# Second layer: its x prepared in eight steps over the block ahead, other places for its weights, two conversions per f, fewer remainders on GpSimd

## The chip, the cores and the metric

The kernel runs on one core of a Trainium2 chip. The metric is the time of one execution on the device in microseconds (us), median of three runs: 994.25 for the kernel before (991.24 to 998.31).

## What is computed

A two-scale attention feeds two feed-forward layers. All matrices are float32 (q, k, v of 4 x 8 x 576 x 64; 2304 tokens of width 512; first layer 512 to 1536 to 512 with a gate, second 512 to 2048 to 512).

```python
q_d = q.reshape(B, H, S // 4, 4, D).mean(axis=3)          # k_d and v_d alike
out_d = softmax(q_d @ k_d.T / 8) @ v_d                    # coarse
scores = where(abs(i - j) < 4, q @ k.T / 8, -1e9)         # a band of 7 keys
x = repeat(out_d, 4) + softmax(scores) @ v                # 2304 x 512
x = (sigmoid(x @ w_gate) * (x @ w_val)) @ w_out           # first layer
h = x @ w_in
out = (h * sigmoid(1.702 * h)) @ w_out2                   # second layer
```

## The kernel before

Each float32 product is made of three TensorE passes: an operand is split into a high part (a cast to the float32r format, on ScalarE) and a remainder (value minus high part, on VectorE or GpSimd), and high x high, remainder x high and high x remainder are summed in PSUM (`passes`, L777 to L779). `parts_of` (L721 and the cast at L719) makes the split and takes the engine of the remainder as an argument.

The tokens are in five blocks: four of 512 tokens, one per batch, and a fifth, E, of the 4 x 64 tokens left over, 256 wide. The first layer visits them in the order 0, 1, 2, E, 3, with the attention of the next batch beside blocks 0 to 2; the second in the order 0, 1, 2, 3, E. In the first layer one step of the loop over d_ff (an f, 128 columns) has a gate product, a value product (both into a PSUM tile `ph`), an evaluation (tanh on ScalarE, L820; the multiplication `th` on VectorE, L825, which reads PSUM), the split of the result (`ghi`, `glo`, L828 and L829), and the output product of the f before. Each f uses three weight tiles of 128 x 512, which are kept in SBUF from the first block on (ring `w`, 36 tiles) and split anew for each block into rings of four tiles, `whi` and `wlo`. `weights` (from L737) says which engine takes the remainder: in block E every other one VectorE and GpSimd, in block 3 VectorE for the output weights (part 2) and GpSimd for the rest.

In the second layer two f's go together (a pair; eight pairs per block) and the product x @ w_in of a block of 512 tokens is made with Strassen's seven products (`hidden2`). For this x is needed as seven sums of quarters, each with high part and remainder (t1, t3, t4, t6 in `xhi` and `xlo`; t7, b11, b22 in tiles `xe0` to `xe2`), and each pair of weight tiles as four pieces (s1; s5 and s2; a11 and a22; s6 and s7), sums at L872, L874 and L877 into the two buffers of ring `we`, and then split into `whi` and `wlo`. `load_x7` prepares the sums of x for a block at one time in the plan, in two halves (k = 0, 1): each reads two tiles of x from DRAM (`st`, two buffers, `x2d`), makes four sums into the tile `tails` (L1028, L1030) and one into a buffer of `we` (L1035) on VectorE, seven casts on ScalarE and seven remainders of 128 x 256 on GpSimd.

The weights arrive as 64 bit words and are converted on the chip (`bits`, L696 to L710): a DMA, a ScalarE operation into a buffer of `we` (L701), and three VectorE operations (L703, L705, L710). `convert2` does this for the second layer's 32 tiles: the 16 tiles of w_in into the ring `raw`, the 16 of w_out into places `w2`, with a split besides. `CONV` says at which f of the first layer's last two visits (E, then 3) which tile is converted; six of w_in are converted in the first three pairs of the second layer's block 0.

Places: the raw tiles `wr0` to `wr7` (`low`) lie under the last 16 of the first layer's 36 weight tiles, and `places` are tiles under the attention's tiles (14) and under the first 20 weight tiles (10), which come free when their first user has ended.

Nothing of the order is written by hand. `Plan.order` takes the operations with an engine, a cost and a due time each, and simulates the five queues: whichever engine is free next takes the operation with the earliest due time among those whose inputs it believes ready. The engines then run these lists in order, and wait on semaphores where an operation's inputs are late. The planner's cost of an operation does not depend on what another engine does at that time.

```python
def parts_of(m, hi, lo, due, eng, n=512):
    (rm, vm), (rh, vh), (rl, vl) = m, hi, lo
    op("act", act_ns(n), lambda: nc.scalar.copy(vh(), vm()), [rm], [rh], due)
    ns, on = (dve_ns(n), nc.vector) if eng == "dve" else (pool_ns(n), nc.gpsimd)
    op(eng, ns, lambda: on.tensor_sub(vl(), vm(), vh().bitcast(F32)), [rm, rh], [rl], due)
```

## Time and profile before

| | |
|---|---|
| median of 3 runs | 994.25 us (991.24 to 998.31) |
| the profiled execution: its time | 996.08 us |
| the profiled execution: its span | 993.9 us |
| granted TensorE clock, mean over the span | 0.974 of full speed |
| TensorE busy | 952.5 us, 96% |
| VectorE busy | 709.1 us, 71% |
| ScalarE busy | 509.8 us, 51% |
| GpSimd busy | 371.6 us, 37% |

PE is TensorE's matmuls, PEld its weight loads, DVE VectorE, ACT ScalarE, POOL GpSimd, SP the queue that issues the DMAs. Times of rows count from the start of the span. A matmul's end is modelled, so that consecutive ones overlap in the rows; what counts is the distance from start to start. A row of the timeline has start, duration, engine, line, operation, tiles (output <- inputs, without buffer numbers), shapes, count, and in brackets the idle time of the engine before it with what ended it. In the stages of the run the first layer's block E begins near 425 us, its block 3 near 482, the second layer near 573, and the second layer's blocks 1, 2 and 3 near 670, 760 and 850.

### The profile page before, as it was taken

Reading aid. Unit: us, or ns where it says so; the run is one execution under the profiler, and the core shown is the slowest. Engines: PE = TensorE matmul, PEld = TensorE weight load, DVE = VectorE, ACT = ScalarE, POOL = GpSimd, SP = SyncE. Lnnn points to the kernel's source line nnn. Section 1 sums busy time; section 2 is a strip of 40 time slices with the busy share of each in tenths; the row PEclk is TensorE's granted clock in tenths of the full one; section 3 lists DMA queues with packets and bytes.
Section 4 is the critical chain, followed back from the end, with each engine's and each line's share of the span. In section 5 each row is a group of like instructions: output and inputs, shape, how many; then the busy total and the mean of one; then the engine's idle time right before and its main releaser. Section 6 shows DMA issues by size and latency. Waiting matters only on the chain.

```text
span 993.9 us, 20546 instructions
## 1 busy us (share of the span) xinstructions
PE 952.5 (96%) x8188; PEld 808.3 (81%) x8188; DVE 709.1 (71%) x1326; ACT 509.8 (51%) x1156; POOL 371.6 (37%) x356
## 2 busy tenths in 40 slices
...
GB/s 212 189 124 198 206 166 190 96 53 81 26 1 123 89 2 2 22 137 14 127 22 168 108 106 85 1 22 65 1 12 12 64 1 22 64 1 1 4 40 22
DMA packets 34447, 71.50 MB, mean 72 GB/s; under 512 B 3448, under 2 KB 15152, under 8 KB 34352
## 3 DMA queue, kind: packets, MB, share of 16 engines
...
## 4 chain that ended last, share of the span: by engine, by line
PE 72%; DVE 16%; issue 4%; DMA 3%; ACT 3%; POOL 1%; SPq 0%; DVEq 0%; ACTq 0%; POOLq 0%
PE ph L777 11%; PE ph L778 10%; PE ph L779 10%; PE acc L777 9%; PE acc L779 9%; PE acc L778 9%; PE pa L778 3%; PE pa L779 3%; PE pa L777 3%; DVE we L705 2%; PE pa L639 2%; DVE w L903 1%; DVE tails L1030 1%; DVE wlo L721 1%; DMA st<-x2d 1%
## 5 line engine op out<-in xcount | busy, mean ns | idle before, releaser
L777 PE MATMUL ph<-xhi,whi 128*128 128x512 f32 (+1 forms) x544 | 200.8, 369 | 3.9 <-DVE th L825 2.7
L778 PE MATMUL ph<-xhi,wlo 128*128 128x512 f32 (+1 forms) x544 | 196.5, 361 | 0.0
L779 PE MATMUL ph<-xlo,whi 128*128 128x512 f32 (+1 forms) x544 | 195.9, 360 | 0.0
L721 POOL TENSOR_TENSOR wlo<-wr,whi 128x512 fp32r<-128x512 f32 x78 | 104.4, 1338 | 150.8 <-ACT whi L719 150.4
L721 POOL TENSOR_TENSOR wlo<-we,whi 128x256 fp32r<-128x256 f32 x64 | 68.2, 1065 | 155.6 <-PE pa L779 101.7
L777 PEld LDWEIGHTS ph<-xhi,whi 128*128 128x128 f32 x544 | 103.1, 190 | 26.1 <-issue 8.1
L778 PEld LDWEIGHTS ph<-xhi,wlo 128*128 128x128 f32 x544 | 103.3, 190 | 16.5 <-DVE wlo L721 0.7
L721 POOL TENSOR_TENSOR wlo<-w,whi 128x512 fp32r<-128x512 f32 x52 | 71.4, 1375 | 119.5 <-ACT whi L719 119.5
L779 PEld LDWEIGHTS ph<-xlo,whi 128*128 128x128 f32 x544 | 103.2, 190 | 15.6
L719 ACT CAST whi<-wr 128x512 fp32r<-128x512 f32 x128 | 78.6, 615 | 41.9 <-PE acc L779 16.0
L825 DVE SCALAR_TENSOR_TENSOR th<-th,ph 128x512 f32<-128x512 f32 (+1 forms) x68 | 41.1, 605 | 70.1 <-PE ph L779 56.5
L777 PE MATMUL acc<-ghi,whi 128*128 128x512 f32 (+1 forms) x232 | 87.3, 376 | 0.0
L779 PE MATMUL acc<-glo,whi 128*128 128x512 f32 (+1 forms) x232 | 85.5, 368 | 1.4 <-DVE glo L829 1.4
L719 ACT CAST whi<-w 128x512 fp32r<-128x512 f32 x100 | 61.2, 616 | 49.7 <-PE ph L779 19.2
L778 PE MATMUL acc<-ghi,wlo 128*128 128x512 f32 (+1 forms) x232 | 85.7, 369 | 0.8 <-DVE wlo L721 0.8
L719 ACT CAST whi<-we 128x512 fp32r<-128x512 f32 (+1 forms) x96 | 52.6, 548 | 62.9 <-DVE w L915 23.4
L820 ACT ACTIVATE th<-ph 128x512 f32<-128x512 f32 (+1 forms) x68 | 36.2, 532 | 61.9 <-PE ph L779 61.9
L778 PE MATMUL acc<-w,glo 128*128 128x512 f32 x144 | 56.9, 395 | 1.4 <-DVE glo L941 1.4
L779 PE MATMUL acc<-w,ghi 128*128 128x512 f32 x144 | 57.3, 398 | 0.0
L703 DVE TENSOR_SCALAR we<-we 128x512 int32<-128x512 int32 x68 | 37.8, 556 | 27.0 <-ACT we L701 26.8
L777 PE MATMUL acc<-w,w 128*128 128x512 f32 x144 | 56.9, 395 | 0.0
L778 PE MATMUL acc<-w,w 128*128 128x512 f32 x144 | 56.8, 394 | 0.0
(162 smaller groups left out, 2424.3 us busy)
## 6 DMA issues: line engine op xcount, KB each, us to landing
...
```

What stands on the lines that cost most here:

```text
L639: nc.tensor.matmul(s.t[h * D:(h + 1) * D, q:q + NQ], vt.t[ks, g, v0 + h * D:v0 + (h + 1) * D], tt.t[ks, h, g, :NQ], start=True, stop=True, ...
L703: op("dve", 335.0, lambda: nc.vector.tensor_scalar(e.t, e.t, 3, None, op0=ALU.logical_shift_left), [], [e], due)
L705: op("dve", 602.0, lambda: nc.vector.scalar_tensor_tensor(e.t, words(0), 29, e.t, op0=ALU.logical_shift_right, op1=ALU.bitwise_or), [w], [ ...
L719: op("act", act_ns(n), lambda: nc.scalar.copy(vh(), vm()), [rm], [rh], due)
L721: op(eng, ns, lambda: on.tensor_sub(vl(), vm(), vh().bitcast(F32)), [rm, rh], [rl], due)
L777: nc.tensor.matmul(o, lhi, rhi, start=first, stop=False, skip_group_check=more)
L778: nc.tensor.matmul(o, llo, rhi, start=False, stop=False, skip_group_check=more)
L779: nc.tensor.matmul(o, lhi, rlo, start=False, stop=last, skip_group_check=more)
L820: op("act", act_ns(n, True), lambda h=h: nc.scalar.activation(th.t[:, :n], h.t[:, :n], AF.Tanh, scale=0.5 if layer == 1 else 1.702 / 4.0), ...
L825: op("dve", dve_ns(n), lambda: nc.vector.scalar_tensor_tensor(th.t[:, :n], th.t[:, :n], 1.0, hb[-1].t[:, :n], op0=ALU.add, op1=ALU.mult), ...
L903: out=tq()[:, o], in0=b.t[:, :H], in1=tq()[:, in1], op=alu) if flip else nc.vector.tensor_tensor(
L1030: op("dve", dve_ns(H), lambda p0=p0, p1=p1, fn=fn, i=i, ff=ff: fn(ff()[:, i], p0[0]()[:, p0[1]], p1[0]()[:, p1[1]]), st, [(four, i)], at)
```

## The change

- `load_x7` becomes a generator with eight steps (two sums each, then the one in `we`, then the two halves of the tiles themselves, for k = 0 and 1). `visit` starts it at the first pair of the block ahead and sends it on once per pair; for block 0 of the second layer it starts at f = 2 of the first layer's block 3. Its DMAs lose their earliest time.
- Places: `low` now lies under the first 16 weight tiles of the first layer, whose last use is early in block 3. One set of the tiles `xe`, the two more `ghi`/`glo` buffers and nine of the w_out places are under the attention's tiles; the other set of `xe` and seven w_out places are under the later weights.
- `CONV`: three w_out tiles in block E instead of six; in block 3 all 16 w_in tiles and six of w_out, 22 over twelve f's, where 10 and 10 stood; the last seven w_out tiles one per pair in the second layer's block 0, where six w_in tiles stood in the first three pairs.
- Remainders: in block E all are on VectorE, in block 3 parts 1 and 2; GpSimd keeps block 3's gate weights.

```diff
--- before.py
+++ after.py
@@ -293,9 +293,9 @@
 
     NRAW = NF2 // 2
     NTOP = 3 * NF1 // 2 - NRAW
+    low = [wpools[0].tile([P, 2, 512], I32, name=f"wr{i}", tag=f"wr{i}") for i in range(NRAW)]
     top = [wpools[1].tile([P, 2, 512], I32, name=f"w{i}", tag=f"w{i}") for i in range(NTOP)]
-    low = [wpools[0].tile([P, 2, 512], I32, name=f"wr{i}", tag=f"wr{i}") for i in range(NRAW)]
-    wslots = [Slot(x[:, i]) for x in top + low for i in range(2)]
+    wslots = [Slot(x[:, i]) for x in low + top for i in range(2)]
     plan.ring("w", wslots)
     aslots = []
     for nm, n, shape in (("qt", 2, [P, S + 12]), ("kt", 2, [P, KPAD + S + 5]), ("vt", 2, [P, NG, VC]),
@@ -318,15 +318,16 @@
             late[side] = tc.alloc_tile_pool(name="w2" + side, bufs=1, side=side, reuse_waits="tile")
         return late[side].tile([P, 2, 512], F32R, name=f"w2_{i}", tag=f"w2_{i}")
 
-    places = [Slot(lambda i=i: second(i), aslots if i < NREG else wslots[:2 * NTOP]) for i in range(NREG + NTOP)]
-    plan.ring("raw", [Slot(x, wslots[2 * (NTOP + i):2 * (NTOP + i) + 2]) for i, x in enumerate(low)])
+    places = [Slot(lambda i=i: second(i), aslots if i < NREG else wslots[2 * NRAW:]) for i in range(NREG + NTOP)]
+    plan.ring("raw", [Slot(x, wslots[2 * i:2 * i + 2]) for i, x in enumerate(low)])
 
     NX, NGX = 3, 2
-    plan.ring("w2", places[:NREG] + places[NREG + 2 * NX + NGX:])
+    NR = NREG - NX - NGX
     for n in range(NX):
-        plan.ring(f"xe{n}", places[NREG + n:NREG + 2 * NX:NX])
+        plan.ring(f"xe{n}", [places[n], places[NREG + NF2 - NR + n]])
+    gplaces = places[NX:NX + NGX]
     plan.ring("ex", places[NREG - 2:NREG])
-    gplaces = places[NREG + 2 * NX:NREG + 2 * NX + NGX]
+    plan.ring("w2", places[NX + NGX:NREG + NF2 - NR])
 
     accs = ring("acc", 4, [P, 512], pool=ps)
     hs_ = ring("ph", 2, [P, 512], pool=ps)
@@ -403,9 +404,12 @@
     FIRST = ((-15.0e3, 0.0), (3.5e3, 0.0), (10.0e3, 8.0e3))
 
 
-    CONV = [[[f // 2] if f % 2 else [] for f in range(NF1)], [[f + 6] for f in range(NF1)]]
-    for f, raws in ((8, (0, 1)), (9, (2, 3)), (10, (4, 5, 6)), (11, (7, 8, 9))):
-        CONV[1][f] = [*[f + 6][:f < 10], *[NF2 + n for n in raws]]
+    CONV = [[[f // 3] if f % 3 == 2 and f < 9 else [] for f in range(NF1)], [[] for _ in range(NF1)]]
+    last = []
+    for p in range(NRAW):
+        last += [NF2 + 2 * p, NF2 + 2 * p + 1, *[p + 3][:p + 3 < NR]]
+    for n, x in enumerate(last):
+        CONV[1][n * NF1 // len(last)].append(x)
     NGROW = 7
     visits = []
     clock = T0
@@ -740,11 +744,8 @@
                 w32[f, part] = buf("w")
                 signed(*bits(1, f, part, t - 8000.0), w32[f, part], t - 8000.0)
             m = whole(w32[f, part], F32)
-            nsplit[0] += 1
             eng = "pool"
-            if vi["j"] == E:
-                eng = ("pool", "dve")[nsplit[0] % 2]
-            elif vi["j"] == 0 or part == 2:
+            if vi["j"] in (0, E) or part == 2 or vi["j"] == B - 1 and part:
                 eng = "dve"
         hi, lo = buf("whi"), buf("wlo")
         parts_of(m, whole(hi), whole(lo), t - 4000.0, eng)
@@ -997,7 +998,7 @@
                 r += c
                 pos += c
 
-    def load_x7(j, t):
+    def load_x7(j):
 
 
         H = 256
@@ -1011,36 +1012,57 @@
         for b, nm in zip(more, ("t7", "b11", "b22")):
             x7[nm] = [(b, n) for n in range(4)], lambda b=b: b.t[:, 0], lambda b=b: b.t[:, 1]
         for k in range(2):
-            at = t - 6000.0 + 2000.0 * k
+            c = slice(k * H, (k + 1) * H)
             st = [buf("st") for _ in range(2)]
-            for n in range(2):
-                dma(st[n].t, x2d[j].t[:, k + 2 * n], P * 4 * T, [(x2d[j], k + 2 * n)], [st[n]], at - 5000.0,
-                    at - 14000.0)
-            four, one = buf("four"), buf("we")
-            ff = lambda four=four: four.t
+            four = buf("four")
+            a, b = ((lambda n=n, st=st: st[n].t.rearrange("p (a c) -> p a c", c=H)) for n in range(2))
+
+            def summed(dst, v, p0, p1, fn, at):
+                op("dve", dve_ns(H), lambda: fn(v(), p0[0]()[:, p0[1]], p1[0]()[:, p1[1]]), st, [dst], at)
+
+            def extra(n, m, at):
+                z = more[n]
+                parts_of(m, ((z, k), lambda c=c: z.t[:, 0, c]), ((z, 2 + k), lambda c=c: z.t[:, 1, c]),
+                         at, "pool", H)
+
+            def minus(o, x, y):
+                nc.vector.scalar_tensor_tensor(o, x, -1.0, y, op0=ALU.mult, op1=ALU.subtract)
+
+            add, less = nc.vector.tensor_add, nc.vector.tensor_sub
+            for i, (p0, p1, fn) in enumerate((((a, 0), (b, 1), add), ((a, 1), (b, 1), less), ((b, 0), (a, 0), less),
+                                              ((a, 0), (a, 1), minus))):
+                if i % 2 == 0:
+                    at = yield
+                if i == 0:
+                    for n in range(2):
+                        dma(st[n].t, x2d[j].t[:, k + 2 * n], P * 4 * T, [(x2d[j], k + 2 * n)], [st[n]], at - 9000.0)
+                v = lambda i=i, four=four: four.t[:, i]
+                summed((four, i), v, p0, p1, fn, at)
+                parts_of(((four, i), v), ((xh, (k, i)), lambda c=c, i=i: xh.t[:, i, c]),
+                         ((xl, (k, i)), lambda c=c, i=i: xl.t[:, i, c]), at, "pool", H)
+            at = yield
+            one = buf("we")
             fo = lambda one=one: one.t.bitcast(F32)[:, :H]
-            a, b = ((lambda n=n, st=st: st[n].t.rearrange("p (a c) -> p a c", c=H)) for n in range(2))
-
-            c = slice(k * H, (k + 1) * H)
-            for i, (p0, p1, fn) in enumerate((
-                    ((a, 0), (b, 1), nc.vector.tensor_add), ((a, 1), (b, 1), nc.vector.tensor_sub),
-                    ((b, 0), (a, 0), nc.vector.tensor_sub),
-                    ((a, 0), (a, 1), lambda o, x, y: nc.vector.scalar_tensor_tensor(
-                        o, x, -1.0, y, op0=ALU.mult, op1=ALU.subtract)))):
-                op("dve", dve_ns(H), lambda p0=p0, p1=p1, fn=fn, i=i, ff=ff: fn(
-                    ff()[:, i], p0[0]()[:, p0[1]], p1[0]()[:, p1[1]]), st, [(four, i)], at)
-                parts_of(((four, i), lambda i=i, ff=ff: ff()[:, i]),
-                         ((xh, (k, i)), lambda c=c, i=i: xh.t[:, i, c]),
-                         ((xl, (k, i)), lambda c=c, i=i: xl.t[:, i, c]), at, "pool", H)
-            op("dve", dve_ns(H), lambda b=b, fo=fo: nc.vector.tensor_add(fo(), b()[:, 0], b()[:, 1]),
-               [st[1]], [one], at)
-            for z, m in zip(more, ((one, fo), (st[0], lambda a=a: a()[:, 0]), (st[1], lambda b=b: b()[:, 1]))):
-                parts_of(m, ((z, k), lambda z=z, c=c: z.t[:, 0, c]),
-                         ((z, 2 + k), lambda z=z, c=c: z.t[:, 1, c]), at, "pool", H)
+            summed(one, fo, (b, 0), (b, 1), add, at)
+            extra(0, (one, fo), at)
+            at = yield
+            extra(1, (st[0], lambda a=a: a()[:, 0]), at)
+            extra(2, (st[1], lambda b=b: b()[:, 1]), at)
+
+    steps = [None]
+
+    def step_x7(at):
+        if steps[0]:
+            try:
+                steps[0].send(at)
+            except StopIteration:
+                steps[0] = None
+
+    def start_x7(j):
+        steps[0] = load_x7(j)
+        next(steps[0])
 
     def load_x(layer, j, t):
-        if layer == 2 and j != E:
-            return load_x7(j, t)
         n = width(j)
         if layer == 1:
             xs[layer, j] = (buf("ex"), buf("ex"))
@@ -1081,6 +1103,11 @@
             else:
                 gh, gl, t = hidden(vi, f, t)
                 g = gh, gl
+
+            if (layer, j) == (1, B - 1) and f == 2 or layer == 2 and j < B - 1 and f == 0:
+                start_x7(j + 1 if layer == 2 else 0)
+            if (layer, j) == (1, B - 1) or layer == 2 and j < B - 1:
+                step_x7(t + 3000.0)
             if pend[0]:
                 t = pend[0](t)
             now[0] = t
@@ -1101,9 +1128,8 @@
                         for x in gplaces:
                             for n, nm in enumerate(("ghi", "glo")):
                                 plan.rings[nm][0].append(Slot(lambda x=x, n=n: x.t[:, n], x.under))
-                if vi["layer"] == 2 and vi["j"] == 0 and f + 11 < NF2:
-                    for n in range(2):
-                        convert2(NF2 + f + 10 + n, t + 1300.0)
+                if vi["layer"] == 2 and vi["j"] == 0 and NR + f // 2 < NF2:
+                    convert2(NR + f // 2, t + 1300.0)
                 return t
 
             pend[0] = fin
```

The planner's lists before and after, at three places. First VectorE at the second layer's step from block 0 to block 1. `wr_112` (before) and `wr_102` (after) are the first raw tile, whose pieces block 1's first pair needs; L874 and L875 sum the pieces s5 and s2 of a pair, and the remainder `wlo` behind is theirs; `th_97<-th_97,w_85` is the last evaluation of block 0. Before:

```order
L1035 TENSOR_TENSOR we_87<-st_101 128x256
L938 SCALAR_TENSOR_TENSOR th_97<-th_97,w_85 128x512
L941 TENSOR_TENSOR w_20_6026<-th_96,w_20_6026 128x512
L874 TENSOR_TENSOR we_86<-wr_113 128x512
L941 TENSOR_TENSOR w_21_6078<-th_97,w_21_6078 128x512
L874 TENSOR_TENSOR we_87<-wr_112 128x512
L721 TENSOR_TENSOR wlo_79<-we_87,whi_75 128x512
```

After:

```order
L904 TENSOR_TENSOR w_85<-w_85,pa_161 128x256
L875 TENSOR_TENSOR we_87<-wr_102 128x512
L904 TENSOR_TENSOR w_85<-w_85,pa_162 128x256
L878 TENSOR_TENSOR we_86<-wr_102 128x512
L725 TENSOR_TENSOR wlo_79<-we_87,whi_75 128x512
L939 SCALAR_TENSOR_TENSOR th_97<-th_97,w_85 128x512
L873 TENSOR_TENSOR we_87<-wr_103 128x256
L942 TENSOR_TENSOR w_4_6064<-th_97,w_4_6064 128x512
```

The remainder of the first pair's s5 and s2 stood behind the evaluation, two splits and another pair's sum; it now stands ahead of the evaluation.

GpSimd from the start of block E of the first layer (`w_13<-tails` are the remainders of E's own x; `w_1_4796` and the like are places of w_out; rows with `st` or `xlo` are the second layer's x). Before:

```order
L1065 TENSOR_TENSOR w_13_4763<-tails,w_12_4756 128x256 x4
L721 TENSOR_TENSOR wlo_79<-w_104,whi_75 128x512
L721 TENSOR_TENSOR w_1_4796<-we_87,w_1_4796 128x512
L721 TENSOR_TENSOR wlo_81<-w_103,whi_77 128x512
L721 TENSOR_TENSOR wlo_81<-w_105,whi_77 128x512
L721 TENSOR_TENSOR wlo_79<-w_106,whi_75 128x512
L721 TENSOR_TENSOR wlo_81<-w_107,whi_77 128x512
L721 TENSOR_TENSOR w_3_4953<-we_87,w_3_4953 128x512
L721 TENSOR_TENSOR wlo_79<-w_108,whi_75 128x512
L721 TENSOR_TENSOR wlo_81<-w_109,whi_77 128x512
L721 TENSOR_TENSOR wlo_79<-w_110,whi_75 128x512
```

After, down to the first remainder of block 3's weights, `wlo_81<-wr_102`:

```order
L1087 TENSOR_TENSOR w_13_4760<-tails,w_12_4753 128x256 x4
L725 TENSOR_TENSOR w_1_4844<-st_100,w_1_4844 128x256
L725 TENSOR_TENSOR w_2_4877<-st_101,w_2_4877 128x256
L725 TENSOR_TENSOR w_6_4900<-we_87,w_6_4900 128x512
L725 TENSOR_TENSOR xlo_90<-tails,xhi_88 128x256 x4
L725 TENSOR_TENSOR wlo_81<-wr_102,whi_77 128x512
```

The weights' remainders are gone from GpSimd here, and half of the x of the second layer's block 0 is prepared at this early place.

VectorE between two evaluations `th` of the first layer's block 3. Before, ahead of the evaluation of f = 7:

```order
L721 TENSOR_TENSOR wlo_80<-wr_113,whi_76 128x512
L710 SCALAR_TENSOR_TENSOR we_86<-w_82,we_86 128x512
L829 TENSOR_TENSOR glo_94<-th_96,ghi_92 128x512
L703 TENSOR_SCALAR we_87<-we_87 128x512
L721 TENSOR_TENSOR w_22_5760<-we_86,w_22_5760 128x512
L705 SCALAR_TENSOR_TENSOR we_87<-w_83,we_87 128x512
L710 SCALAR_TENSOR_TENSOR wr_112<-w_83,we_87 128x512
L703 TENSOR_SCALAR we_86<-we_86 128x512
L705 SCALAR_TENSOR_TENSOR we_86<-w_84,we_86 128x512
L710 SCALAR_TENSOR_TENSOR wr_112<-w_84,we_86 128x512
L703 TENSOR_SCALAR we_87<-we_87 128x512
L705 SCALAR_TENSOR_TENSOR we_87<-w_82,we_87 128x512
```

After, from f = 0 to the evaluation of f = 1:

```order
L725 TENSOR_TENSOR wlo_78<-wr_104,whi_74 128x512
L830 TENSOR_TENSOR glo_94<-th_96,ghi_92 128x512
L714 SCALAR_TENSOR_TENSOR wr_103<-w_84,we_86 128x512
L707 TENSOR_SCALAR we_87<-we_87 128x512
L709 SCALAR_TENSOR_TENSOR we_87<-w_85,we_87 128x512
L707 TENSOR_SCALAR we_86<-we_86 128x512
L980 TENSOR_SCALAR ev_99<-acc_158 128x256
L714 SCALAR_TENSOR_TENSOR wr_103<-w_85,we_87 128x512
L725 TENSOR_TENSOR wlo_80<-wr_105,whi_76 128x512
L709 SCALAR_TENSOR_TENSOR we_86<-w_82,we_86 128x512
L1021 TENSOR_TENSOR we_87<-st_101 128x256
L826 SCALAR_TENSOR_TENSOR th_97<-th_97,ph_160 128x512
```

Stretches of this length (twelve or thirteen instructions) stood ahead of the evaluations of f = 7, 8 and 9 before, with six to eight instructions in the others; in the list of the change eight of the nine from f = 0 to f = 9 have eleven to fourteen, and the last two have four and five.

## Rows read from the trace of the kernel before

**Rows 1.** The page, busy us (share of the span) and instructions of each engine

```profile
PE 952.5 (96%) x8188; PEld 808.3 (81%) x8188; DVE 709.1 (71%) x1326; ACT 509.8 (51%) x1156; POOL 371.6 (37%) x356
```

**Rows 2.** Windows by stage: length, busy us (instructions) of PE, PEld, DVE, ACT, POOL, PEclk

```profile
424.70:482.00 57.30, 55.31 (x428) 53.22 (x427) 50.58 (x67) 36.55 (x75) 33.38 (x24) 1.00 0.19 61
482.00:548.00 66.00, 66.00 (x293) 54.66 (x292) 44.58 (x64) 35.50 (x65) 29.14 (x23) 1.00 0.34 120
548.00:572.60 24.60, 20.72 (x89) 16.21 (x88) 22.17 (x28) 12.03 (x26) 18.60 (x17) 1.00 0.32 106
572.60:664.00 91.40, 84.24 (x500) 72.50 (x500) 84.61 (x150) 48.87 (x106) 36.81 (x33) 0.98 0.18 58
664.00:753.00 89.00, 86.24 (x526) 77.31 (x527) 68.54 (x133) 46.90 (x104) 40.19 (x40) 0.98 0.08 25
753.00:842.00 89.00, 86.62 (x531) 77.65 (x530) 69.06 (x133) 46.72 (x104) 40.21 (x40) 0.98 0.08 25
842.00:931.00 89.00, 85.27 (x531) 76.38 (x530) 64.13 (x127) 44.62 (x98) 34.88 (x33) 1.00 0.06 19
931.00:994.00 63.00, 57.77 (x344) 50.62 (x343) 29.23 (x51) 23.86 (x55) 9.07 (x7) 0.99 0.08 26
```

**Rows 3.** PE's timeline where the second layer's blocks 1, 2 and 3 begin

```profile
672.18 0.28 PE L778 MATMUL ph<-xhi,wlo 128*128 128x256 f32 x1
672.30 0.28 PE L779 MATMUL ph<-xlo,whi 128*128 128x256 f32 x1
674.78 0.39 PE L777 MATMUL pa<-w,whi 128*128 128x256 f32 x1 [2.20 <-ACT whi L719]
675.50 0.58 PE L778 MATMUL pa<-w,wlo 128*128 128x256 f32 x1 [0.34 <-DVE wlo L721]
675.88 0.41 PE L779 MATMUL pa<-w,whi 128*128 128x256 f32 x1
...
763.84 0.54 PE L777 MATMUL pa<-w,whi 128*128 128x256 f32 x1 [1.97 <-ACT whi L719]
...
853.83 0.39 PE L777 MATMUL pa<-w,whi 128*128 128x256 f32 x1 [3.04 <-ACT whi L719]
```

**Rows 4.** Timeline of DVE and ACT ahead of the stall at 674.78

```profile
669.87 0.68 DVE L938 SCALAR_TENSOR_TENSOR th<-th,w 128x512 f32<-128x512 f32 x1
...
671.63 1.23 DVE L874 TENSOR_TENSOR we<-wr 128x512 f32<-128x512 f32 x1
...
673.39 0.68 DVE L874 TENSOR_TENSOR we<-wr 128x512 f32<-128x512 f32 x1
...
674.11 0.62 ACT L719 CAST whi<-we 128x512 fp32r<-128x512 f32 x1 [2.60 <-DVE we L874]
```

**Rows 5.** DVE's timeline in the first layer's block 3

```profile
519.86 0.68 DVE L825 SCALAR_TENSOR_TENSOR th<-th,ph 128x512 f32<-128x512 f32 x1
...
528.01 0.68 DVE L825 SCALAR_TENSOR_TENSOR th<-th,ph 128x512 f32<-128x512 f32 x1
...
537.76 0.68 DVE L825 SCALAR_TENSOR_TENSOR th<-th,ph 128x512 f32<-128x512 f32 x1
538.36 0.69 DVE L721 TENSOR_TENSOR wlo<-wr,whi 128x512 fp32r<-128x512 f32 x1
...
540.62 1.67 DVE L705 SCALAR_TENSOR_TENSOR we<-w,we 128x512 int32<-128x512 int32 x1
...
549.52 0.68 DVE L825 SCALAR_TENSOR_TENSOR th<-th,ph 128x512 f32<-128x512 f32 x1
```

**Rows 6.** POOL's timeline at the same place

```profile
540.38 1.36 POOL L721 TENSOR_TENSOR w<-we,w 128x512 fp32r<-128x512 f32 x1 [4.95 <-ACT w L719]
541.69 1.75 POOL L721 TENSOR_TENSOR wlo<-wr,whi 128x512 fp32r<-128x512 f32 x1
```

**Rows 7.** The chain of waits ahead of block 1: start, us, what

```profile
659.70 2.90 DMA st<-x2d
```

**Rows 8.** Waits of ACT's conversions: us in total, times, longest

```profile
ACT we L701 <- DMA w<-w: 10.7, 6, 5.7
```

## The prediction

> **What bounds the kernel now.** I read the page first: TensorE is busy for 952.5 of 993.9 us, no other engine for more than 71% [rows 1]. So the time is TensorE's, and a change that moves no matmul can only win where TensorE stands still. The windows by stage say where that is. From block E of the first layer to the end of the second layer's block 3 the length less PE's busy time is 2.0, 0.0 and 3.9, 7.2, 2.8, 2.4 and 3.7 us: together 22.0 [rows 2]. The stretch before 424.7 us is hardly touched by the change, and of the 5.2 us after 931 most is the last output's way out.
>
> The idle time of the rows is not all that a stall costs. At the start of the second layer's block 1 the matmuls go 0.12 us from start to start (672.18, 672.30); then come 674.78, 675.50 and 675.88 [rows 3]. That is 3.58 us for three that would take 0.36, so 3.2 lost, where the brackets say 2.20 and 0.34. I therefore price a us of idle time at 3.2 / 2.54 = 1.3 us.
>
> The same view, around the starts of blocks 2 and 3, shows stalls of 1.97 and 3.04 us, all three released by ACT's cast `whi` [rows 3]. What that cast waited for stands in the timeline of the other two engines: VectorE makes the last evaluation of block 0 at 669.87, then two splits and two sums L874, and only the second sum, at 673.39, is the one whose cast starts at 674.11 [rows 4]. It is the order that holds it back: both `we` buffers were taken, one by L1035 of x. Further back the chain of waits begins with a load of x, 2.90 us [rows 7].
>
> In block 3 of the first layer I read VectorE's evaluations `th`. They come 8.15 us apart (519.86, 528.01), which is TensorE's time for one f; at the end of the block 11.76 us apart (537.76, 549.52) [rows 5]. There the list has thirteen instructions instead of seven, and some are slow: L705 takes 1.67 us while GpSimd's remainder runs, where 0.69 us is usual for a wide one without it (L721 at 538.36) [rows 5, 6].
>
> **What GpSimd costs VectorE.** A wide (128 x 512) VectorE instruction takes 0.60 us from start to start (537.76 to 538.36) [rows 5]; for a narrow one, and for the shift L703, I take the 0.34 that follows if some 0.08 us of it does not depend on the width (an estimate). Between the same marks the list before has, in block E, 34 wide and 30 narrow: 30.6 us. VectorE was busy for 50.6, with three instructions more, and GpSimd for 33.4 [rows 2]: some 18 us too much, 0.5 us for each us of GpSimd. Block 3: 65 and 27, 48.2 us against 44.6 + 22.2, GpSimd 29.1 + 18.6: 0.39. Block 0 of the second layer: 67 and 80, 67.4 us (three more rows in the window) against 84.6, GpSimd 36.8: 0.44. These ratios hold whatever the mechanism is.
>
> The Trainium skill has the rule (SBUF — State Buffer, Who interferes with whom): a VectorE instruction with two SBUF inputs and a GpSimd instruction that reads SBUF want one port pair, and the loser is blocked for the winner's whole instruction. L705 against 0.69 us agrees. Taken to its end, each GpSimd us as a VectorE us, block 0 would need 67.4 + 36.8 = 104 us of VectorE before; the window measured 84.6, so half of the overlaps miss one another, and I keep the ratios.
>
> **The change part by part.** No matmul is added or taken away.
>
> *Boundaries in the second layer.* The list now has the first pair's remainder of s5 and s2 ahead of the last evaluation; it stood behind it, behind two splits and another pair's sum. The lists at the next two boundaries differ in the same way. The 2.20, 1.97 and 3.04 us should go, and most of what follows them. What is late next is GpSimd: the second half of x still ends in the last pair (three of its five sums, four of its remainders), among that pair's other remainders. I leave 1.5 of 8.9 us idle over the three blocks: 7.4 x 1.3 = 9.6 us won. Range: 11.6 (all) to 4.8 (half).
>
> *Block 3.* The list has 81 wide and 30 narrow instead of 65 and 27: 58.8 us, since remainders came from GpSimd, 16 instead of 10 raw tiles are converted (six more by three instructions) and four w_out tiles fewer. GpSimd has 23 instead of 44, 15 wide and 8 narrow; at 1.36 us for a wide one [rows 6] and 0.75 for a narrow one (an estimate, a little over half of it), that is 26 us, at 0.39 another 10. VectorE: 69 us, before 66.8, so it is no lighter, but even. The heaviest f has 7.0 us and about 0.9 from GpSimd, 7.9 of 8.15 us; before, three in a row had 7 us while GpSimd was busy 18.6 of 24.6 us. I take 1.5 us idle instead of 3.9: 3.1 us won. Range: 5.0 won to 3 lost, if the stretches of 7 us meet more than their share of GpSimd.
>
> *Block 0 of the second layer.* 66 wide and 80 narrow, 66.8 us, where 67.4 stood; GpSimd has 19 wide and 23 narrow instead of 16 and 18, 43 instead of 35 us, at 0.44 another 3.4 us for VectorE. So this block gets no lighter either: 66.8 + 0.44 x 43 = 86 us of its 8 x 11.1 (the starts of blocks 1 and 2 are 89.1 us apart [rows 3]). But its pairs, which had 11.2, 11.3, 6.4 and 10.7 us behind the first and then 7.0 to 8.5, now have 8.2, 9.7, 10.8, 5.8, 9.7, 9.5, 10.7 and 7.3. With GpSimd's share (1.9 us per pair before, 2.4 now) less 11.1, VectorE's lag, pair by pair, rose before to 2.0 and 4.1, on top of a first pair of 9.5 that met the end of block 3; now it is 0, 1.0, 3.1, 0.2, 1.2, 2.0, 4.0. Part of that is caught by what is ready ahead. I take 4.0 us idle instead of 7.2: 4.2 us won. Range: 8 won to 3 lost.
>
> *Block E.* GpSimd loses all 18 weight remainders and VectorE gets them: 47 wide and 32 narrow, 39.1 us instead of 30.6. With GpSimd down to seven instructions the total falls from 50.6 to some 42. But both halves of other work meet at the start: E's own four remainders, a conversion and half of the x for the second layer stand together, and VectorE's first five f's have 17.0 instead of 13.9 us against 5 x 4.1 of TensorE (half of 8.15). With 4 to 5 us from GpSimd that is 21 to 22 of 20.5. I add 1.0 us idle: 1.3 us lost. Range: 2 won to 4 lost.
>
> *At nothing.* The places as such: the same loads and stores. The x loads on SP's queue lose their earliest time; two go up in the list between the stores of the first layer's block 0, whose landing they wait for, with the next heads' q and k behind them. TensorE has attention and the weights of a whole block there; if that cover failed, one wait would cost at most about the 2.90 us of such a load [rows 7]. The others leave earlier than before, which removes that wait at the boundaries.
>
> **Sum.** 996.08 (the profiled execution, 993.9 of it span) - 9.6 - 3.1 - 4.2 + 1.3 = 980.5. This execution was 1.8 us over the median of the three runs, so the forecast is 978.7, in round figures 979.
>
> **Rivals.**
> 1. *Only the boundaries gain.* VectorE is as busy in blocks 3 and 0 as before, and if being even is worth nothing, only 9.6 is won and 1.3 lost: 994.25 - 8.3 = 986. For it: the total loads, 69 against 66.8 and 86 against 84.6. Against it: the stalls stood in the f's and pairs with most work, and none in 482 to 548 [rows 2].
> 2. *The x is still late.* The steps don't go where they are asked for: the planner takes x in two lumps, in pairs 2 to 3 and 6 to 7, and the last remainders are GpSimd's business at the boundary. Then half of the 9.6 stays: 978.7 + 4.8 = 983.5. Against it: the cast that released all three stalls doesn't wait for x.
> 3. *Slower: conversions block ScalarE.* In block 3 two conversions per f share two `we` buffers, with x's own sum besides, and ScalarE's conversion (L701) waits in order for a buffer or a load, with the casts `whi` of the weights queued behind it; TensorE waits for those. It waited for loads six times before, 10.7 us in all, 5.7 at the longest [rows 8]. With 22 conversions in a row, half of them holding ScalarE for that mean of 1.8 us with nothing in stock would cost 20 us and eat the 3.1: 978.7 + 23 = 1002. It decides from a wait of some 3 us on: four buffers `whi` hold a third more than the three tiles of an f, which is 8.15 / 3 = 2.7 us of work in stock. Against it: ScalarE is at 35.5 of 66 us there [rows 2].
>
> On the other hand the Trainium skill warns (Perfetto Trace Analysis, Optimizing Scalar/DVE Operations) that shifting work between VectorE and GpSimd may not help, as they share a read port. In block E the rows go against it: a remainder costs GpSimd over 1.3 us, hence VectorE some 0.7, and on VectorE 0.6; by the warning block E would be worth nothing, which is within its range.
>
> **Chances.** Forecast 0.61, the first rival 0.17, the second 0.15, the third 0.07. Measurements tell 1% from no change here, that is 984.3 and 1004.2. Faster: 0.57 of the forecast, 0.09 of the second rival, 0.05 of the first, 0.71. Slower by over 1%: about half of the third and a little of unseen things, 0.06. The rest, 0.23, is within 1%. The range: below, all stalls gone, 22.0 x 1.3 = 28.6, would be 966, and I stop at 967; above, rival 1 (986) with the losses that bound block E (2.7 more) and part of those of block 3, 991.
>
> **What would show it.** Right: no wait of PE for ACT's `whi` over 1 us at the three boundaries; evaluations in block 3 about 8.2 us apart throughout; GpSimd busy below 10 us in block E; idle PE of 5 to 8 us in all from block E to block 3. Wrong: stalls at the boundaries released by GpSimd's `wlo` (rival 2), evaluations of block 3 or pairs of block 0 regularly late with VectorE busy without a gap (rival 1), waits of ScalarE's conversion for buffers or loads with PE behind them (rival 3), or a stall of 3 us and more at the start of block E.

## The result and the profile after

The changed kernel takes 983.04 us (median of 4 runs, 980.24 to 985.63), the kernel before beside it 993.65 (991.24 to 998.31): a ratio of 0.9887, interval 0.9840 to 0.9934. The forecast was 979, range 967 to 991, "faster". The gain was there, 11 us of the 15 foretold. That it lies in the range is in part luck: two of the four terms of the sum had the wrong sign, one each way, and the time is that of the second rival (983.5), whose reason came at one boundary of three.

The page of the changed kernel, busy us, against [rows 1]: GpSimd has 36 us less, VectorE 1 us more with 30 instructions more.

```profile
PE 943.9 (96%) x8188; PEld 803.2 (82%) x8188; DVE 710.1 (72%) x1356; ACT 510.5 (52%) x1156; POOL 335.5 (34%) x326
```

The windows of the changed kernel, columns as in [rows 2]; the cuts are put at evaluations `th`, so that a stage can be compared whatever came ahead of it: block E (from the last evaluation of block 2 to the first of block 3), block 3, the end of the first layer, then the second layer's blocks 0 to 3 (from one block's first wide `th` to the next one's).

```profile
410.20:473.10 62.90, 62.87 (x520) 60.42 (x520) 52.58 (x93) 43.17 (x90) 14.52 (x14) 1.00 0.22 76
473.10:563.40 90.30, 88.51 (x395) 73.20 (x394) 75.28 (x115) 47.78 (x88) 31.73 (x22) 1.00 0.37 123
563.40:576.50 13.10, 11.78 (x70) 9.95 (x69) 12.81 (x18) 8.35 (x20) 11.90 (x10) 1.00 0.16 61
576.50:678.70 102.20, 92.16 (x527) 79.53 (x526) 96.01 (x160) 55.46 (x120) 52.04 (x43) 0.95 0.12 41
678.70:762.20 83.50, 82.58 (x521) 74.48 (x520) 66.19 (x133) 45.70 (x103) 38.36 (x38) 1.00 0.08 25
762.20:847.40 85.20, 84.27 (x528) 75.88 (x527) 64.75 (x129) 46.05 (x102) 36.56 (x36) 1.00 0.09 26
847.40:920.60 73.20, 73.20 (x461) 66.07 (x460) 49.34 (x105) 36.45 (x79) 22.32 (x20) 1.00 0.04 15
```

The same windows of the kernel before, for its second layer's blocks 0 to 3:

```profile
586.70:683.40 96.70, 88.31 (x514) 76.83 (x515) 86.53 (x155) 50.76 (x112) 42.56 (x40) 0.96 0.14 46
683.40:772.20 88.80, 86.42 (x529) 77.49 (x528) 68.79 (x133) 46.76 (x105) 40.05 (x38) 0.98 0.08 25
772.20:861.90 89.70, 85.75 (x531) 76.59 (x530) 70.63 (x133) 48.02 (x109) 43.76 (x42) 1.00 0.10 30
861.90:934.40 72.50, 72.50 (x458) 65.51 (x457) 49.32 (x105) 36.30 (x78) 22.31 (x20) 1.00 0.04 16
```

Block E has no stall left, blocks 1 and 2 are 5.3 and 4.5 us shorter. Block 0 is 5.5 us longer, and VectorE is busy in it for 96.0 of 102.2 us, where it had 86.5 of 96.7. Over these seven rows the length less PE's busy time is 15.0 us, where it was 22.0 [rows 2]. The marks give the whole account, in us:

| from, to | before | after | difference | foretold |
|---|---|---|---|---|
| start to the first evaluation | 66.5 | 62.8 | -3.7 | 0 |
| to the last of block 2 | 347.6 | 347.5 | -0.2 | 0 |
| block E, to the first of block 3 | 66.0 | 62.9 | -3.1 | +1.3 |
| block 3, to its last | 94.1 | 90.3 | -3.8 | -3.1 |
| end of the layer and block 0 | 109.3 | 115.3 | +6.0 | -4.2 |
| blocks 1 to 3 | 251.0 | 241.9 | -9.1 | -9.6 (with the start of block 1) |
| to the end | 59.5 | 59.4 | -0.1 | 0 |

The first line is not counted as the change's. In the profiles of the eleven kernels below the first evaluation stands anywhere from 60.8 to 67.6 us, though nothing ahead of it was edited. Without it the profiled executions differ by 10.2 us, the medians by 10.6.

The marks have a flaw: the change moves the evaluations themselves, since VectorE's list now has a remainder ahead of the last one of a block. TensorE's own rows don't move. These are the first product of the second layer, the first of its block 1, and an output product near the end of its block 3; before, then after:

```profile
575.54 0.28 PE L777 MATMUL ph<-xhi,whi 128*128 128x256 f32 x1
670.27 0.28 PE L777 MATMUL ph<-xhi,whi 128*128 128x256 f32 x1
934.83 0.39 PE L778 MATMUL acc<-w,glo 128*128 128x512 f32 x1
```

```profile
566.02 0.28 PE L778 MATMUL ph<-xhi,whi 128*128 128x256 f32 x1
664.30 0.28 PE L778 MATMUL ph<-xhi,whi 128*128 128x256 f32 x1
921.04 0.39 PE L779 MATMUL acc<-w,glo 128*128 128x512 f32 x1
```

By these, everything from the first evaluation to the second layer gains 5.8 us (not 7.1), block 0 loses 3.6 (not 6.0 with the end of the layer), and block 1 to the end of block 3, the start of block 1 included, gains 7.8 (not 9.1). The windows between the first two, before and after, hold the same 517 products:

```profile
575.54:670.27 94.73, 87.57 (x517) 75.50 (x516) 88.17 (x156) 51.24 (x112) 42.47 (x38) 0.98 0.17 56
```

```profile
566.02:664.30 98.28, 89.96 (x517) 77.64 (x516) 92.25 (x155) 54.46 (x119) 50.66 (x44) 0.95 0.15 49
```

Where TensorE still waits (its rows of the changed kernel, stalls over 1 us from block E on):

```profile
503.26 0.47 PE L778 MATMUL ph<-xhi,whi 128*128 128x512 f32 x1 [1.79 <-DVE th L826]
593.68 0.39 PE L778 MATMUL pa<-w,whi 128*128 128x256 f32 x1 [1.33 <-ACT whi L723]
615.70 0.40 PE L778 MATMUL ph<-xhi,whi 128*128 128x256 f32 x1 [2.18 <-DVE w L904]
618.69 0.58 PE L779 MATMUL pa<-w,wlo 128*128 128x256 f32 x1 [1.04 <-DVE wlo L725]
633.52 0.39 PE L778 MATMUL ph<-w,whi 128*128 128x256 f32 x1 [1.02 <-ACT w L898]
667.14 0.38 PE L779 MATMUL pa<-w,wlo 128*128 128x256 f32 x1 [1.24 <-DVE wlo L725]
670.28 0.39 PE L779 MATMUL ph<-xhi,wlo 128*128 128x256 f32 x1 [1.45 <-POOL wlo L725]
```

The waits for `whi` where blocks 2 and 3 began [rows 3] are gone. Four of the seven stalls are in block 0, two of these for VectorE itself; the last two are behind block 1's first product. At 667.14 TensorE waits there for VectorE, and at 670.28 for a remainder on GpSimd that is queued behind four of x (664.23 to 668.82): the second rival, at this one boundary.

### The profile page after: what moved, and what is told of

The parts are those of the page before. It is cut to its first block, busy times and chain, and to the rows that moved or that the text cites. A ratio compares the mean times of both kernels' runs of the same rounds, so it can differ in the third digit from the quotient of the medians.

```text
span 980.0 us, 20528 instructions
## 1 busy us (share of the span) xinstructions
PE 943.9 (96%) x8188; PEld 803.2 (82%) x8188; DVE 710.1 (72%) x1356; ACT 510.5 (52%) x1156; POOL 335.5 (34%) x326
## 4 chain that ended last, share of the span: by engine, by line
PE 77%; DVE 15%; issue 3%; ACT 2%; POOL 2%; DMA 1%; SPq 0%; DVEq 0%; ACTq 0%
PE ph L778 11%; PE ph L779 11%; PE ph L780 11%; PE acc L778 10%; PE acc L779 9%; PE acc L780 9%; PE pa L779 3%; PE pa L780 3%; PE pa L778 3%; DVE we L709 2%; PE pa L643 2%; DVE wlo L725 1%; PE pa L531 1%; DMA vg<-v 1%; DVE wr L714 1%
## 5 line engine op out<-in xcount | busy, mean ns | idle before, releaser
L725 POOL TENSOR_TENSOR wlo<-wr,whi 128x512 fp32r<-128x512 f32 x70 | 97.4, 1392 | 166.3 <-ACT whi L723 164.1
L725 POOL TENSOR_TENSOR wlo<-we,whi 128x256 fp32r<-128x256 f32 x64 | 67.9, 1060 | 138.2 <-PE pa L780 102.7
L723 ACT CAST whi<-we 128x512 fp32r<-128x512 f32 (+1 forms) x96 | 52.6, 548 | 51.4 <-DVE w L916 23.8
L725 POOL TENSOR_TENSOR wlo<-w,whi 128x512 fp32r<-128x512 f32 x30 | 40.1, 1336 | 112.9 <-ACT whi L723 112.9
L709 DVE SCALAR_TENSOR_TENSOR we<-w,we 128x512 int32<-128x512 int32 x68 | 57.4, 845 | 0.4
L725 DVE TENSOR_TENSOR wlo<-w,whi 128x512 fp32r<-128x512 f32 x70 | 49.4, 707 | 10.5 <-ACT whi L723 9.9
L780 PE MATMUL acc<-w,w 128*128 128x512 f32 x144 | 57.0, 396 | 0.0
```

Of the source, the lines that this page charges most:

```text
L709: op("dve", 602.0, lambda: nc.vector.scalar_tensor_tensor(e.t, words(0), 29, e.t, op0=ALU.logical_shift_right, op1=ALU.bitwise_or), [w], [ ...
L780: nc.tensor.matmul(o, lhi, rlo, start=False, stop=last, skip_group_check=more)
```

## Experiments

Nine start from the changed kernel, two from the kernel before. A ratio is against the kernel before beside it (medians 996 to 998 us). The changed kernel was not run beside them, so a difference to its 983.04 is one of separate runs; those named below show in the profiles too (first evaluation to last wide one: 857.8 us in the changed kernel). The theory to be tested: VectorE is what TensorE waits for in block E, block 3 and block 0, and a remainder that GpSimd makes costs VectorE at least what it saves it. The rivals: the number and the place of conversions and steps.

**Block E's remainders back on GpSimd.**

```diff
-            if vi["j"] in (0, E) or part == 2 or vi["j"] == B - 1 and part:
+            nsplit[0] += 1
+            if vi["j"] == E:
+                eng = ("pool", "dve")[nsplit[0] % 2]
+            elif vi["j"] == 0 or part == 2 or vi["j"] == B - 1 and part:
```

> The changed kernel, but in block E of the first layer the weights' remainders alternate between GpSimd and VectorE again, as in the kernel before. In the changed kernel block E (last evaluation of block 2 to the first of block 3) took 62.9 us, before 66.0. Theory 1, the remainders did it (GpSimd's instructions stretch VectorE's by more than VectorE would need for them): the block goes back to about 66 us and the kernel is some 3 us slower than the changed one, 986 for 983. Theory 2, it is the three conversions fewer that block E now has (3 for 6): the block stays at 63 us or falls below, VectorE being relieved of 18 remainders, and the kernel stays at 983.

990.69 us, ratio 0.9948 (0.9917 to 0.9978), more than the 986 of the first theory. Block E takes 69.1 us, more than before. One instruction shows what happens to VectorE: `glo` of block E, the evaluation's remainder, always on VectorE, its width and count the same. First the kernel before, then this experiment, then the changed kernel (us in all, mean ns):

```profile
L829 DVE TENSOR_TENSOR glo<-th,ghi 128x256 fp32r<-128x256 f32 x12 | 11.1, 924 | 2.5 <-ACT ghi L828 2.5
```

```profile
L833 DVE TENSOR_TENSOR glo<-th,ghi 128x256 fp32r<-128x256 f32 x12 | 10.6, 884 | 1.0 <-ACT ghi L832 1.0
```

```profile
L830 DVE TENSOR_TENSOR glo<-th,ghi 128x256 fp32r<-128x256 f32 x12 | 5.5, 459 | 0.0
```

The remainders make block E's gain, not the three conversions fewer. VectorE has 78 instructions and is busy for 55.0 us with GpSimd beside it; it has 93 and 52.6 us without.

**The kernel before with the new remainders alone**, the rule of blocks E and 3.

> The kernel before with one part of the change alone: in block E all remainders of weights on VectorE, in block 3 of the first layer those of parts 1 and 2. Before, block E took 66.0 us and block 3 94.1. Theory 1, in block E the gain is the remainders alone: 62.9 us, as in the changed kernel, 3 us won. In block 3 the conversions remain crowded into its last four f's, where VectorE gets a third wide remainder per f and GpSimd loses one: by 0.56 us per us of GpSimd that is even, so 93 to 95 us. The second layer stays as it was: 990 to 992 for the 994 to 996 of the kernel before. Theory 2, the gain needs the new places and conversions as well: within 1 us of before.

989.35 us, ratio 0.9931 (0.9904 to 0.9958). Block E 63.5 us, block 3 92.6: -2.5 and -1.5, 4.0 of the change's 6.9 us there; the rest came with the conversions and places together, which no run takes apart. The stalls at the boundaries of the second layer are untouched (2.20, 1.96 and 3.04 us).

**Block 0 of the second layer without GpSimd.**

```diff
-            parts_of(m, (hi, seen(hi)), (lo, seen(lo)), at, eng, n)
+            parts_of(m, (hi, seen(hi)), (lo, seen(lo)), at, "dve" if vi["j"] == 0 else eng, n)
...
-                 due, "pool" if f % 2 else "dve")
+                 due, "pool" if f % 2 and f < NR else "dve")
...
-                         ((xl, (k, i)), lambda c=c, i=i: xl.t[:, i, c]), at, "pool", H)
+                         ((xl, (k, i)), lambda c=c, i=i: xl.t[:, i, c]), at, "dve" if j == 1 else "pool", H)
```

> The changed kernel, but in block 0 of the second layer GpSimd makes no remainders: those of the pieces, of the w_out conversions and of block 1's x go to VectorE. In the changed kernel the eight pairs (first wide evaluation of block 0 to the first of block 1) took 102.2 us; VectorE was busy for 96.0 of them, GpSimd for 52.0. VectorE's 66 wide and 80 narrow instructions would be 66.8 us alone. Theory 1, the block is VectorE's and GpSimd costs it 0.56 us per us: 21 wide and 22 narrow remainders more at 0.60 and 0.34 make 87 us, with nothing left to stretch them, so the eight pairs take 92 to 94 us and the kernel 974 to 976. Theory 2, the loss of this block is the place of the steps and GpSimd hides most of what it does: VectorE then has 20 us more to do in the same pairs, the eight pairs take 102 to 110 us, the kernel 983 to 991. The prediction's ratio of 0.44 gives 90 us for 87, some 3 us won: 980.

973.85 us, ratio 0.9772 (0.9747 to 0.9797): 9 us below the changed kernel. The eight pairs take 95.6 us for 102.2, a little more than the 92 to 94 of the first theory. VectorE has 193 instructions for 160 and is busy for less:

```profile
577.40:673.00 95.60, 88.48 (x527) 76.27 (x526) 93.62 (x193) 54.92 (x117) 13.20 (x11) 1.00 0.13 43
```

**Block 0 without its conversions** (`convert2` takes an earlier tile for f >= NR, so that seven w_out tiles are left out and the output is another; the run is for its time alone).

> The changed kernel with the seven w_out tiles that block 0 of the second layer converts left out (their loads, conversions and splits; the second layer then uses earlier tiles in their places). VectorE was busy for 21.7 us with them, GpSimd for 5.9. Theory 1, the eight pairs of 102.2 us are VectorE's whole work: without them VectorE has some 71 us, less than TensorE's 89, the stalls go and the pairs take 89 to 91 us, the kernel 970 to 973. Theory 2, it is x and its remainders on GpSimd that hold the pairs 3 and 7 up: these two pairs stay over 13 us and the kernel is at 978 or more.

965.07 us. The eight pairs take 83.1 us, none over 11.1, with x and its remainders still on GpSimd:

```profile
578.60:661.70 83.10, 82.72 (x517) 73.90 (x516) 67.88 (x133) 46.44 (x105) 42.45 (x39) 1.00 0.08 23
```

With 67.9 us of VectorE in 83 GpSimd's 42.5 us hold nothing up, with 96 in 102 they do. So the block is as long as VectorE's whole load, and not as a few late remainders of x.

**Block 1's x late**: all eight steps in block 0's last pair.

> The changed kernel, but block 1's x is not taken in eight steps over block 0: all eight steps stand in its last pair, so that by the list VectorE has 17 to 20 instructions in each of the pairs 1 to 6, and the x (seven sums, fourteen remainders on GpSimd) stands in pairs 6, 7 and the first of block 1. Theory 1, block 0 is limited by VectorE's whole work: the eight pairs take 102 us as before, or more, as GpSimd's remainders now all stand at the boundary; the kernel 982 to 988. Theory 2, the loss comes from conversions and steps that meet in one pair (pair 3 took 16.3 us, pair 7 14.5): the pairs 1 to 6 fall to 11 or 12 us each, the boundary loses 2 to 4 us, and the kernel is at 976 to 979.

983.12 us. Pairs 1 to 7 take 11.2, 11.8, 10.6, 13.3, 11.7, 9.8 and 11.1 us, and the first of block 1 21.3. The second theory was right on the seven pairs, but the eighth takes what they gain and the sum stays (100.9 for 102.2): where in the block the work stands is worth next to nothing while the block is VectorE's.

**x asked for as before, in all blocks.**

> The changed kernel with the second layer's x asked for as before: all of a block's x due 6 and 4 us ahead of the block, its loads at most 14 us earlier. By the list x then stands in the pairs 4 to 7, and block 0's pairs have 8.5 to 9.5 us of VectorE each, evenly, where the changed kernel had 6.1 to 11.0. Theory 1, the eight steps removed the stalls at the boundaries: these come back, 2 to 3 us at each of blocks 1, 2 and 3, and the kernel takes 6 to 9 us more than the changed one, 989 to 992, however even block 0 is. Theory 2, the boundaries gained by the order of the conversions and weights and not by the steps: they stay free of stalls over 1 us, block 0 gains from its evenness, and the kernel is at 978 to 983.

990.47 us, ratio 0.9933 (0.9908 to 0.9958): 7.4 us lost. Blocks 1 and 2 take 86.3 and 91.0 us (83.5 and 85.2), with stalls at their ends:

```profile
754.51 0.58 PE L778 MATMUL ph<-w,whi 128*128 128x256 f32 x1 [2.99 <-ACT w L898]
844.60 0.58 PE L778 MATMUL ph<-w,whi 128*128 128x256 f32 x1 [4.04 <-ACT w L898]
```

So the eight steps do remove the boundaries' stalls, while GpSimd is at work.

**The second layer without GpSimd**, the edit of block 0 for all blocks and conversions; then block 3 of the first layer too.

> The changed kernel with GpSimd making no remainders of the second layer at all: its pieces, all w_out conversions (also those in block E and block 3 of the first layer), the x of blocks 0 to 3 and the weights of the second layer's block E are VectorE's. Leaving GpSimd out of block 0 alone gave 973.9 us. Theory 1, GpSimd costs VectorE about what it saves, and the gain comes only where VectorE is the limit: blocks 1, 2 and 3 have no stall to lose (85, 85 and 80 us between their outputs, VectorE busy for three quarters) and stay as they are, the first boundary gains what GpSimd held there, 1 to 2 us, so 972 to 974. Theory 2, the narrow stage of a pair needs both engines: by the list VectorE then has 8.7 to 11.0 us in the pairs of blocks 1 and 2, of TensorE's 10.6, and these blocks take 88 us and more: 977 to 981.

> The kernel without GpSimd in the second layer, and block 3 of the first layer gives GpSimd's remaining twelve remainders (part 0 of every f) to VectorE too. In the changed kernel block 3 took 90.3 us from its first evaluation to its last, for TensorE's 88; its f's 2 and 3 were 10.3 and 11.1 us apart instead of 8.2, with x on GpSimd, and VectorE was busy for 74.4 of 87.6 us. Theory 1 (GpSimd's us costs VectorE 0.4 to 0.56): VectorE's list grows to 58.8 + 11.7 = 70.5 us with nothing to stretch it, the late f's come in 8.2 to 9 us, block 3 takes 88 to 89 us, the kernel 1 to 2 us less than without this edit: 971 to 973. Theory 2: the late f's are the conversions' own work, and stay at 10 and 11 us: no change.

965.46 us, ratio 0.9681 (0.9641 to 0.9722), and 968.12, ratio 0.9702 (0.9667 to 0.9737), which is the same (840.3 and 840.7 us from the first evaluation to the last wide one). The first is the best kernel here with the whole output, 17.6 us below the changed one. It is better than its own forecast, as two places gained that the run without GpSimd in block 0 had left: the last two pairs of block 0 (19.6 us for 26.1) and block 3 (88.2 for 90.3). The f's 2 and 3 of block 3, 10.3 and 11.1 us after one another in the changed kernel, come in 8.1 and 8.0 where the remainders of x and conversions are VectorE's. Block 0's row, and some instructions in it (us in all, mean ns):

```profile
571.30:660.10 88.80, 84.17 (x509) 73.37 (x509) 86.95 (x190) 52.28 (x112) 0.00 (x0) 1.00 0.14 45
```

```profile
L709 DVE SCALAR_TENSOR_TENSOR we<-w,we 128x512 int32<-128x512 int32 x7 | 4.8, 683 | 0.0
L707 DVE TENSOR_SCALAR we<-we 128x512 int32<-128x512 int32 x7 | 2.9, 418 | 0.0
L904 DVE TENSOR_TENSOR w<-w,pa 128x256 f32<-128x256 f32 x16 | 6.6, 415 | 0.9 <-ACT th L937 0.8
```

and the same lines in the changed kernel's block 0:

```profile
L709 DVE SCALAR_TENSOR_TENSOR we<-w,we 128x512 int32<-128x512 int32 x7 | 10.0, 1433 | 0.0
L904 DVE TENSOR_TENSOR w<-w,pa 128x256 f32<-128x256 f32 x16 | 6.6, 413 | 2.6 <-ACT th L937 2.6
L707 DVE TENSOR_SCALAR we<-we 128x512 int32<-128x512 int32 x7 | 4.8, 680 | 0.7 <-ACT we L705 0.7
```

With no GpSimd in the block the wide VectorE instructions take 0.68 us and the narrow ones 0.42. Beside GpSimd those whose inputs are all in SBUF are longer, L709 twice as long, and L904, which reads PSUM, is not. The shift L707 with its one SBUF input is longer too.

**GpSimd at work for nobody.** Added to the best kernel, in block 1:

```diff
+        for n in range(4 if vi["j"] == 1 and 1 <= p <= 6 else 0):
+            o = buf("ev")
+            op("pool", pool_ns(512), lambda o=o: nc.gpsimd.tensor_sub(o.t, o.t, o.t), [], [o],
+               t + 2500.0 * n, t + 2500.0 * n)
```

> The kernel without GpSimd in the second layer (965.5 us), with 24 wide GpSimd subtractions added in its block 1 on a buffer that nobody reads; only the block's last evictions, several pairs later, wait for it. They have nothing to wait for but the block's start, so they stand one behind the other, some 32 us, while VectorE's list is the same word for word. Theory 1, GpSimd at work stretches VectorE's instructions whatever it computes: those of 0.68 us with two SBUF inputs take 1 us and more beside it, those that read PSUM stay at 0.41; at 0.5 to 0.6 us for each us of GpSimd VectorE needs 16 to 19 us more in a stretch in which it had some 2 to spare, so the kernel takes 978 to 984. Theory 2, the cost of GpSimd was only the latency of its results, for which others waited: VectorE's durations stay and the kernel is at 965.

983.46 us: 18.0 lost, by work whose results nobody uses; VectorE's list is the same, instruction by instruction. GpSimd's timeline (its first subtraction, ahead of the stretch and beside VectorE instructions that read PSUM, the stretch of 28.9 us, and one of that stretch by itself), then VectorE's beside it, then a PSUM reader in the stretch:

```profile
671.22 1.04 POOL L884 TENSOR_TENSOR ev<-ev 128x512 f32<-128x512 f32 x1 [119.66 <-ACT whi L723]
674.20 28.85 POOL L884 TENSOR_TENSOR ev<-ev 128x512 f32<-128x512 f32 x22 [0.82 <-DMA out<-ev]
678.38 1.49 POOL L884 TENSOR_TENSOR ev<-ev 128x512 f32<-128x512 f32 x1
```

```profile
678.89 1.52 DVE L878 TENSOR_TENSOR we<-wr 128x512 f32<-128x512 f32 x1
680.34 1.52 DVE L947 TENSOR_TENSOR w<-th,w 128x512 fp32r<-128x512 f32 x1
681.78 1.25 DVE L1026 TENSOR_TENSOR tails<-st,st 128x256 f32<-128x256 f32 x1
682.96 1.52 DVE L725 TENSOR_TENSOR wlo<-we,whi 128x512 fp32r<-128x512 f32 x1
```

```profile
L909 DVE TENSOR_TENSOR w<-w,pa 128x256 f32<-128x256 f32 x2 | 0.8, 408 | 0.0
```

From start to start a wide VectorE instruction takes 1.45 us instead of 0.60, and a narrow one with SBUF inputs 1.18 instead of 0.34: each that follows another of its kind loses 0.85 us, whatever its width (the few behind a PSUM reader lose less). In these 28.9 us GpSimd makes 22 instructions, and VectorE just 22 whose inputs are in SBUF: here the two engines take turns. GpSimd pays as well, 1.49 us beside a wide instruction for 1.04 undisturbed. So the price is 0.85 us of VectorE for one such subtraction that finds VectorE with such work waiting, and VectorE would make a wide remainder itself in 0.60. A wide remainder of this kernel takes GpSimd 1.28 us at the least, more than this subtraction of a tile from itself; its price in such a stretch was not measured.

**What is left of the change without GpSimd**: the kernel before, and the one with x asked for as before, each with the second layer's remainders on VectorE.

> The kernel before, with none of the change, but with the second layer's remainders (pieces, w_out conversions, x, weights of its block E) all on VectorE. The same edit took the changed kernel from 983 to 965.5 us. Theory 1, the change's own gains stand beside that of GpSimd: block E keeps its weights' remainders on GpSimd (3 us), the casts at the boundaries still wait for sums that stand behind the x (2 us and more at each of three), by the list the last pair of each block has 11.5 to 15 us of VectorE: the kernel gains 8 to 12 us, as block 0 does, and is at 983 to 987. Theory 2, the boundaries' stalls were GpSimd's stretching of VectorE as well, and what is left to the change is block E and block 3: 970 to 974.

> The changed kernel without GpSimd in the second layer (965.5 us) with x asked for as before, all of it due at the end of the block ahead. With GpSimd at work the same edit cost 7.4 us (990.5 for 983.0). By the list the last pair of block 0 then has 16.1 us of VectorE, those of blocks 1 and 2 11.9, TensorE 10.5. Theory 1, the steps' gain is the order and stands without GpSimd too: 5 to 8 us more, 970 to 974. Theory 2, the boundaries' stalls came from GpSimd's long remainders of x there: within 2 us of 965.5.

974.16 us, ratio 0.9764 (0.9738 to 0.9791), and 971.32, ratio 0.9738 (0.9713 to 0.9763). The kernel before gains 23.4 us by this edit alone, twice what the change gained. Its blocks 1, 2 and 3 take 83.1, 84.8 and 70.1 us, without a stall over 1 us (nor is there one at the start of block 1, where the longest is 0.82):

```profile
672.30:755.40 83.10, 83.10 (x519) 74.78 (x518) 75.60 (x169) 46.17 (x103) 0.00 (x0) 1.00 0.04 11
755.40:840.20 84.80, 84.80 (x533) 76.49 (x531) 78.25 (x172) 47.28 (x107) 1.68 (x2) 1.00 0.10 32
```

The planner made the list anew, but the sums L874 still stand behind the last evaluation, two splits and all of x (741.43 to 746.59 ahead of block 2). So x late costs nothing at these two boundaries once GpSimd is silent, and the second theory holds there. The second of the two kernels still pays at the end of block 0, by the first theory: end of the layer and block 0 take 100.7 us with the steps and 108.3 without, where the last pair has 16.1 us of VectorE by the list; 3.3 us of this come back in blocks 1 to 3.

## Why the prediction was right, and where not

*TensorE's stalls are the gain: right.* All but 0.3 of the 10.2 us came between block E and block 3 of the second layer, where TensorE's idle time fell by 7 us, so that a us of it was worth some 1.4 (1.3 foretold). But 15.0 us stayed, for the 5 to 8 that were to show the forecast right and the 10 that its own terms add up to (3.0, 1.5, 4.0 and 1.5); 10.0 of them are in block 0.

*Boundaries, 9.6 foretold: 7.8 by TensorE's products, and half right in cause.* The stalls of 1.97 and 3.04 us went; the same products come 4.1 and 4.5 us earlier for it. The start of block 1 gained only 0.6: what block 0 is late lands there, with a wait for VectorE (1.24 us) and one for GpSimd's queue of x (1.45). "It is the order that holds it back" was one half: with x asked for as before, the stalls come back. The other was the stretching, to be seen in [rows 4] as the first L874 of 1.23 us for 0.68: without GpSimd x asked for as before has no stall over 1 us at these starts. Either cure was enough.

*Block 3, 3.1 foretold: right in size.* 3.8 measured, 1.5 of it by the remainders alone. But the evaluations are not "about 8.2 us apart throughout": the f's 2 and 3, where x begins, are 10.3 and 11.1 us apart. The second of these is the third rival, see below.

*Block E, 1.3 lost foretold, 3.1 won: the sign was wrong.* The step that failed is "both halves of other work meet at the start ... 21 to 22 of 20.5". The totals ahead of it (39.1 us of list instead of 30.6, some 42 busy instead of 50.6) were the better guide: measured 52.6 with 93 instructions of the whole block, for 56.1 with 77 before. The start, counted against TensorE's pace to the microsecond, has more in stock than that: the 12 us from 419 to 431 are full of VectorE, and TensorE does not wait.

*Block 0, 4.2 won foretold, 3.6 lost by TensorE's products: the sign was wrong.* The step that failed is the one from "no lighter" to "4.2 us won": that the same work, spread more evenly over the pairs, leaves TensorE idle for less. VectorE was busy for 88.2 of 94.7 us before and for 92.3 of 98.3 after, and without its conversions the eight pairs take 83. So the block is as long as VectorE's work, 4.1 us more of it made it 3.6 us longer, and where in the block the work stands gave nothing (x late: 100.9 for 102.2). The sum "66.8 + 0.44 x 43 = 86 us" hid this. Its list is too short: 66.8 is for 146 instructions, where the eight pairs have 160, and the prediction's own figures for these pairs add up to 71.7. And GpSimd was busy for 52.0 us instead of 43, as its own instructions are stretched too (a narrow remainder of x 0.91 us before, 1.16 after). With 71.7 alone the sum is 90.6 us of "8 x 11.1", a block that is over-full.

The ratio itself stood. At the prediction's prices the instructions between TensorE's two products are 69.6 us before (65 wide, 90 narrow) and 69.5 after (66 and 88), which leaves 0.44 and 0.45 us per us of GpSimd. (The 0.56 of the expectations above is (96.0 - 66.8) / 52.0, with the list that is too short; with 71.7 it is 0.47.) But "these ratios hold whatever the mechanism is" goes too far: in the changed kernel's blocks 1 and 2 the same reckoning gives 0.23.

*The port rule.* The prediction weighed the Trainium skill (SBUF — State Buffer, Who interferes with whom: the loser of the shared port pair is blocked for the winner's whole instruction) and kept the averages, since "half of the overlaps miss one another". The experiment beside block 1 is near that rule: one GpSimd instruction, 1.04 us undisturbed, to each of VectorE's, 0.85 us lost. The Trainium skill's warning that shifting work between the two might not help (Perfetto Trace Analysis, Optimizing Scalar/DVE Operations) is borne out, and more: here work that had been shifted to GpSimd cost more than it relieved, and taking back the second layer's share gave 17.6 us.

*Rivals.* The first (being even is worth nothing) was right for block 0, the second at one boundary of three. The third came once, behind the stall of 1.79 us at 503.26 in block 3:

```profile
494.39 4.06 POOL L725 TENSOR_TENSOR wlo<-wr,whi 128x512 fp32r<-128x512 f32 x1 [4.73 <-ACT whi L723]
499.55 1.29 POOL L725 TENSOR_TENSOR w<-we,w 128x512 fp32r<-128x512 f32 x1
500.88 0.67 ACT L705 ACTIVATE we<-w 128x512 f32<-128x512 f32 x1 [3.15 <-POOL w L725]
501.58 0.94 DVE L707 TENSOR_SCALAR we<-we 128x512 int32<-128x512 int32 x1 [2.59 <-ACT we L705]
```

ScalarE's conversion waits 3.15 us for a buffer of `we`, which a remainder on GpSimd frees. VectorE, whose list has the shift of this conversion ahead of the evaluation, is idle for 2.59 us, and TensorE waits for the evaluation. That remainder was late because the one ahead of it took 4.06 us. Here GpSimd was the one held: VectorE made six instructions in a row from 494.14 to 497.30, each at its usual 0.41 or 0.68 us.

What stays open: what makes the start differ, 60.8 to 67.6 us to the first evaluation. No run was made for it. The granted clock differs with it: its mean up to the first evaluation is 0.69 in the profile before and 0.78 in the changed kernel's, with TensorE busy for 53.3 and 47.9 us. The three shortest starts have 0.75 to 0.78, but a start of 62.9 us has 0.67.
